# Loading and preparing a pair's q and k three steps sooner, and giving v a norm and a scale of its own, in a fused attention and two-stage MoE kernel

## The chip, the core and the metric

The kernel runs on one core of a Trainium2 chip. The metric is the time of one execution in microseconds (us), and lower is better. The core's engines are TensorE (PE in the profile, with PEld for its weight loads), VectorE (DVE), ScalarE (ACT), GpSimd (POOL) and SyncE (SP). Each runs its own instructions in the order in which they were issued. SP and POOL mostly start transfers (DMAs) here.

## The reference, cut to what matters

```python
B, H, S, D = 4, 8, 576, 64
q_rot, k_rot = rotate(q), rotate(k)                 # rope
scores = q_rot @ k_rot.T / sqrt(D)                  # 576 x 576 for each of 32 heads
attn = softmax(scores)
x = (attn @ v)                                      # -> 2304 tokens x 512
h = x @ w_in; x = leaky(h) @ w_out                  # dense MoE stage, 512 -> 2048 -> 512
logits = normalize(x) @ normalize(expert_emb).T / tau
out = gate * relu(x @ w1[e]) @ w2[e]                # second stage, one of 8 experts per token
```

All inputs and outputs are float32. The kernel reaches that precision by splitting numbers into a high and a low part (float16 or a rounded float32) and adding the products. To fit float16, a tensor is first scaled by a power of two, which is found from its sum of squares.

## The kernel before

**Pairs, units and steps.** Two heads make a pair, and there are 16 pairs (`g`), four for each batch. A pair is cut into nine units (`u`), blocks of query rows. One call of `step(i)` issues one step: the scores of unit i+1 (`a_scores`, lines 570 to 574), the maximum of unit i (`a_max`, line 579), the exponential and the two parts of P of unit i-1 (`a_exp` 584, `a_hi` 588, `a_lo` 592), the transpose of that P by a DMA on SP's queue (`a_transpose`, line 596, tile PT), and the product with v of unit i-4 (`a_pv`, line 631). The first four pairs (`WHOLE`) are computed in full float32 and transpose with PE instead; pairs 4 to 15 are split, and only they have `prep`, `prep_v` and the DMA transposes.

**The dense stage in between.** Once x of two blocks of 128 tokens is complete, units of the dense stage are issued in the same steps: `m_s1` (line 256, one in every second step) and `m_s2` (line 286) in the step after it. A block's x gets there by `x_done`: a square on ACT, a power of two on DVE, two halves `x16` (lines 684 and 686) and a DMA transpose on SP's queue (line 690, tiles xT and xt). After attention the rest of the dense stage, the routing and the experts follow.

**Preparing a pair.** `load(g, 2)` brings q and k of a pair (640 KB) by one DMA on POOL's queue into the only buffer `raw2`; `load(g, 1)` brings v (320 KB) into `raw1`. `prep(g)` is a list of pieces:

- the squares of q, k and v (line 461, ACT) with rope (lines 389, 392, 396, DVE);
- `total` (line 186), a PE product with ones that adds the three sums over the partitions;
- `_pow2` (lines 91 to 93) and two small products (lines 470, 471) on DVE, which give the scales;
- the high parts (line 482, ACT) and the low parts (line 486, DVE) with one copy (line 512) into `stg`;
- a DMA transpose of `stg` into `stk` on SP's queue (line 515), and two DMAs of 80 KB on POOL's queue that copy q's rows into `zq` (line 523). These wait for the transpose, and behind them on POOL's queue stands `load(g + 1, 2)`.

`prep_v(g)` then makes v's high and low parts (lines 535, 537) with the third scale of the same `_pow2`, copies them to other partitions by two DMAs of 130 and 162.5 KB on POOL's queue (lines 540, 541), and issues `load(g + 1, 1)` behind them.

**What sets the order.** With i0 = 9 (g - 1), the step at which the pair before begins, the first piece of `prep(g)` may run from step i0 - EARLY, and at the soonest TLOAD = 4 steps after its load was issued. The transpose into `stk` may run from step i0 - 1. `prep_v`'s first piece runs from step i0 + LAG = i0 + 4. `slot` takes the pieces of the waiting jobs: x_done first, then prep, prep_v, routing, and weights last. A step has two such places (four before the dense stage begins), with one piece of a job in each; a job that changes its engine, or that needs PE, waits for the next step. `prep(g)` is created only when both its q and k and its v have been asked for.

Of the kernel before, what the change touches and what calls it, by code (L numbers as in the profile page):

```python
# [9 lines left out]
F32 = mybir.dt.float32  # L10
# [32 lines left out]
BUR = 1.5
WARM = 9
# [39 lines left out]
            self.run()  # L84


def _pow2(nc, pool, sq2, n, inv):

    t = pool.tile([128, n], U32, name="pt", tag=f"pt{n}")
    s = pool.tile([128, n], F32, name="ps", tag=f"ps{n}")  # L90
    nc.vector.tensor_scalar(out=t, in0=sq2.bitcast(U32), scalar1=0xFFFFFFFF, scalar2=24, op0=ALU.bitwise_xor, op1=ALU.logical_shift_right)
    nc.vector.tensor_scalar(out=s.bitcast(U32), in0=t, scalar1=-50.0, scalar2=2.0 ** 23, op0=ALU.add, op1=ALU.mult)
    nc.vector.tensor_scalar(out=inv.bitcast(U32), in0=t, scalar1=-2.0 ** 23, scalar2=304.0 * 2 ** 23, op0=ALU.mult, op1=ALU.add)
    return s


# [1 line left out]
def attention_moe_kernel(ctx: ExitStack, tc: tile.TileContext, qkv, w_in, w_out, emb, tau, w1, w2,  # L98
                         rope, ident, tokc, iota, pcol, out):
    nc = tc.nc  # L100
# [66 lines left out]
    M = Ctx()  # L167
# [36 lines left out]
    def weights(i):  # L204
        while len(slices) > (SPARE if i >= NW else 0):
            f, o = slices.popleft()
            if i < NW:
                raw = wp.tile([128, 512, 2], U32, name=f"raw{i}")
            else:
                raw = mp.tile([128, 8, 256], F16, name="xT", bufs=XTB).rearrange("p a b -> p (a b)").bitcast(U32).rearrange("p (f t) -> p f t", t=2)  # L210
            if o:
                nc.sync.dma_start(out=raw.rearrange("p f t -> p (f t)"), in_=w_out32[128 * f:128 * f + 128, :])
                r = yield from decode(raw)
                yield Piece(A=0.75, when=lambda: f in M.scaled)
                nc.scalar.activation(out=wo[:, 0, f], in_=r, func=AF.Copy, scale=uw[:, f:f + 1])
                yield Piece(V=0.6)
                nc.vector.scalar_tensor_tensor(out=wo[:, 1, f], in0=r, scalar=uw[:, f:f + 1], in1=wo[:, 0, f].bitcast(F32), op0=ALU.mult, op1=ALU.subtract)
            else:
                nc.sync.dma_start(out=raw.rearrange("p (c f) t -> p c (f t)", c=4),
                                  in_=w_in32[:, 256 * f:256 * f + 256].rearrange("(c p) f -> p c f", p=128))  # L220
                w = yield from decode(raw)
                sq = small.tile([128, 1], F32, name="wsq", bufs=NW)
                yield Piece(A=0.86)
                nc.scalar.activation(out=junk[:, 0:512], in_=w, func=AF.Square, accum_out=sq, saturate=False)
                pb = yield from total(sq, 1)
                yield Piece(must=True, V=0.2)
                s = _pow2(nc, small, pb[:, 0:1], 1, uw[:, f:f + 1])
                M.scaled.add(f)
                hi = wi[:, 0, :, 128 * f:128 * f + 128]
                wv = w.rearrange("p (c f) -> p c f", c=4)  # L230
                yield Piece(A=0.75)
                nc.scalar.activation(out=hi, in_=wv, func=AF.Copy, scale=s)
                yield Piece(V=0.6)
                nc.vector.scalar_tensor_tensor(out=wi[:, 1, :, 128 * f:128 * f + 128], in0=wv, scalar=s, in1=hi, op0=ALU.mult, op1=ALU.subtract)
            M.wdone[o].add(f)
            yield Piece()
# [119 lines left out]
        nc.gpsimd.memset(e[:, S:640], 0.0)  # L356
    tab = qkp.tile([128, 2, 5, 64], F32, name="tab")
    raws = {}
    pairs, values = {}, {}
    xrow = {}  # L360

    def load(g, z):
        raws[g, z] = qkp.tile([128, z, 5, 2, 64], F32, name=f"raw{z}")
        for t in ([slice(0, 2)] if g else [slice(0, 1), slice(1, 2)]) if z == 2 else [slice(2, 3)]:
            if z == 2:
                M.loaded = M.tick
            if (g, z, t.start) == (0, 2, 1):
                nc.sync.dma_start(out=tab, in_=rope)
            (nc.gpsimd if g else nc.sync).dma_start(out=raws[g, z][:, t.start % 2:t.start % 2 + t.stop - t.start], in_=qkv[g, :, t])
# [84 lines left out]

    def prep(g):
        i0 = 9 * (g - 1)
        raw, rawv = raws.pop((g, 2)), raws.pop((g, 1))[:, 0]
        sq = small.tile([128, 3], F32, name="sq3")

        def square(t):  # L460
            nc.scalar.activation(out=junk, in_=(raw[:, t] if t < 2 else rawv).rearrange("p c h d -> p (c h d)"), func=AF.Square, accum_out=sq[:, t:t + 1], saturate=False)

        by_head = raw.rearrange("p t c h d -> p t h c d")

        m3 = small.tile([128, 3], F32, name="m3")
        sc = small.tile([128, 2], F32, name="sc")

        def scales(pb):
            s3 = _pow2(nc, small, pb[:, 0:3], 3, m3)
            nc.vector.scalar_tensor_tensor(out=sc[:, 0:1], in0=m3[:, 0:1], scalar=0.125, in1=m3[:, 1:2], op0=ALU.mult, op1=ALU.mult)  # L470
            nc.vector.tensor_scalar(out=sc[:, 1:2], in0=sc[:, 0:1], scalar1=-1.0, scalar2=None, op0=ALU.mult)
            return s3
# [19 lines left out]
        yield Piece(A=0.93, V=0.85)  # L492
        square(1)
        rope_s(1)
        yield Piece(A=0.93, V=1.5)
        square(2)
        rope_c(0)
        rope_c(1)
        yield Piece(V=1.4)
        add(slice(0, 2))  # L500
        pb = yield from total(sq, 3)
        yield Piece(must=True, V=0.6)
        s3 = scales(pb)
        s2, qhi, khd, qlo, klo = stacks()
# [5 lines left out]
        yield Piece(V=1.3)  # L510
        lo(klo, 1, khd[:, :, :, 0:64])
        nc.vector.tensor_copy(out=khd[:, :, :, 64:128], in_=khd[:, :, :, 0:64])
        yield Piece(at=i0 - 1)
        stk = stp.tile([128, 5, 640], F16, name="stk")
        nc.sync.dma_start_transpose(out=stk.rearrange("p s (c x) -> p (s c) x", c=5), in_=s2)
# [6 lines left out]
            for h in range(2):  # L522
                nc.gpsimd.dma_start(out=zq[g % 2][64 * h:64 * h + 64, h, 0:640], in_=stk[64 * h:64 * h + 64, h])
        pairs[g] = (stk, s3, sc, zq[g % 2] if zq else None)
        if g + 1 < 4 * B:
            load(g + 1, 2)
        vjobs.append(Job(prep_v(g, rawv, s3)))

    def prep_v(g, rawv, s3):
        yield Piece(A=0.82, at=9 * (g - 1) + LAG)  # L530
        v16 = values[g] = stp.tile([128, 9, 2, 130], F16, name="v16", tag="v")
        nc.gpsimd.memset(v16[:, 0:5, :, 128:130], 1.0)
        vh, vl = (v16[:, 0:5, :, o:o + 64].rearrange("p c h d -> p (c h) d") for o in (64, 0))
        rv = rawv.rearrange("p c h d -> p (c h) d")
        nc.scalar.activation(out=vh, in_=rv, func=AF.Copy, scale=s3[:, 2:3])
        yield Piece(V=0.75)
        nc.vector.scalar_tensor_tensor(out=vl, in0=rv, scalar=s3[:, 2:3], in1=vh, op0=ALU.mult, op1=ALU.subtract)
        yield Piece()

        nc.gpsimd.dma_start(out=v16[0:64, 5:9], in_=v16[64:128, 0:4])  # L540
        nc.gpsimd.dma_start(out=v16[64:128, 4:9], in_=v16[0:64, 0:5])
        if g + 1 < 4 * B:
            load(g + 1, 1)
# [89 lines left out]

    def a_fin(g, u, o):
        b, p = divmod(g, 4)
        s3 = pairs[g][1]
        c = u // 2
        r = slice(0, 128) if c < 4 else slice(64 * (b % 2), 64 * (b % 2) + 64)
        if c == 4 and b % 2:
# [8 lines left out]
        if g < WHOLE:  # L648
            nc.vector.tensor_scalar(out=rd[r], in0=ov[r, :, 64:65], scalar1=1e-9, scalar2=None, op0=ALU.add)
        else:  # L650
            nc.vector.tensor_scalar(out=rd[r], in0=ov[r, :, 64:65], scalar1=EPS_P, scalar2=s3[r, 2:3], op0=ALU.add, op1=ALU.mult)
        nc.vector.reciprocal(out=rd[r], in_=rd[r])
        nc.vector.tensor_tensor(out=x[r, 128 * p:128 * p + 128].rearrange("p (h d) -> p h d", h=2), in0=ov[r, :, 0:64],
                                in1=rd[r].to_broadcast([n, 2, 64]), op=ALU.mult)
# [17 lines left out]
    def x_done(b, c, x):  # L672
# [1 line left out]
        ch = chunk[b, c]  # L674
        j = block_of[b, c]
        yield Piece(A=0.61, when=lambda: not any(z.live for z in wjobs[NW:]) and j < cur_block() + (2 * XTB if decoded() else XTB))
        sq = small.tile([128, 1], F32, name="xsq")
        nc.scalar.activation(out=junk[:, 0:512], in_=x, func=AF.Square, scale=2.0 ** 0.5, accum_out=sq, saturate=False)
        yield Piece(V=0.5)
        s = _pow2(nc, small, sq, 1, ux[:, ch:ch + 1])  # L680
# [16 lines left out]

    def directions():

        en2 = small.tile([NE, 1], F32, name="en2")  # L700
        warm = small.tile([128, 1], F32, name="warm")
# [341 lines left out]
    L.prep, L.x, L.fin, L.o = None, -1, None, None  # L1043

    def jobs():
        if (L.prep is None or not L.prep.live) and preps and all((preps[0], z) in raws for z in ((2,) if preps[0] < WHOLE else (1, 2))):
            L.prep = Job((prep_whole if preps[0] < WHOLE else prep)(preps.popleft()))
        for q in (xjobs, vjobs, rjobs):
            while q and not q[0].live:
                q.popleft()  # L1050
        return [z for z in [*list(xjobs)[:2], L.prep, *list(vjobs)[:1], *list(rjobs)[:1], *wjobs] if z is not None and z.live]
# [350 lines left out]
```

## Time and profile before

| what | value |
|---|---|
| three timed runs | 1005.59, 1006.17 and 1009.71 us, median 1006.17 us |
| the profiled execution | 1004.24 us |
| its span, from the first instruction to the last | 1002.5 us |
| mean granted clock of TensorE | 0.984 of full speed |
| busy share of the span | PE 92%, DVE 77%, PEld 76%, ACT 67%, POOL 11% |

The span is what the profile's views divide up; 1.7 us of the execution lie around it. A wait that a view names is idle time of one engine, and it costs time only where that engine, or one that waits for it, sets the pace.

### The profile page before, as it was taken

To read this page: it belongs to the slowest core of one execution; us is meant where nothing else is said; L and a number is where in the kernel's file an instruction comes from. 1 tells how busy PE (TensorE), PEld (TensorE's weight loads), DVE (VectorE), ACT (ScalarE), POOL (GpSimd) and SP (SyncE) were. 2 spreads that over 40 slices of the span, in tenths; PEclk is the share of its full clock that TensorE was granted. 3 is DMA by queue.
4 is the path that set the end of the run, shared out by engine and by line. 5 is a ranking of instruction groups with operands and counts; after the bars stand their busy time and mean duration, and the time that the engine had idled before them with its cause. 6 is when DMAs were issued, how large, how long until landed. Compare 5 with 4: busy or idle time off the path is not lost. (4 is left out here: it accounts for less than half of the span.)

```text
span 1002.5 us, 20186 instructions
## 1 busy us (share of the span) xinstructions
PE 922.8 (92%) x7428; PEld 762.3 (76%) x7428; DVE 774.6 (77%) x1632; ACT 671.0 (67%) x1081; POOL 114.8 (11%) x157
## 2 busy tenths in 40 slices
PE   2788977899996999998899999999999999999997
PEld 1677766577885788887778888888877788888885
DVE  5988887787888889888778766322668999999993
ACT  5888888555676866667566655333155998888883
POOL 0000000001101100110100100000012351111111
PEclk9999999899998999999989999999999999999999
DMA  6435442969889998977957744101323111116190
GB/s 233 140 108 164 158 137 65 131 110 146 159 131 165 180 151 140 176 142 133 173 110 138 155 77 86 40 22 33 127 85 106 55 42 53 43 43 211 40 358 25
DMA packets 219848, 120.09 MB, mean 120 GB/s; under 512 B 194711, under 2 KB 203159, under 8 KB 219744
## 3 DMA queue, kind: packets, MB, share of 16 engines
q1 hardware_dynamic: 210000, 84.54, 40.4%
q0 software_dynamic: 9744, 34.21, 13.0%
q8 instruction: 60, 0.98, 0.4%
q14 instruction: 44, 0.36, 0.1%
HBM read 120.04 MB, written 10.49 MB: 130 GB/s over the span
## 5 line engine op out<-in xcount | busy, mean ns | idle before, releaser
L256 PEld LDWEIGHTS <-wi 128*128 128x128 f16 x1920 | 170.4, 98 | 28.0 <-issue 7.3
L286 PE MATMUL acc<-wo,gh 128*128 128x512 f32 x576 | 154.6, 411 | 6.0 <-ACT gh L270 6.0
L263 ACT ACTIVATE g<-h 128x512 f32<-128x512 f32 x72 | 43.0, 597 | 138.3 <-DVE gl L274 64.4
L286 PEld LDWEIGHTS acc<-wo,gh 128*128 128x128 f32 x576 | 105.4, 192 | 30.6 <-ACT gh L270 8.4
L579 DVE TENSOR_SCALAR_CACHE_REDUCE E<-S,sc 128x576 f32<-128x576 f32 x108 | 87.9, 814 | 45.7 <-PE S L572 33.3
L584 ACT ACTIVATE E<-E,amx 128x576 f32<-128x576 f32 x144 | 110.5, 767 | 16.9 <-DVE E L579 16.1
L256 PE MATMUL h<-xT,wi 128*128 128x256 f16 (+1 forms) x1152 | 112.0, 255 | 2.5 <-DMA xT<-x 2.5
L256 PE MATMUL h<-xt,wi 128*128 128x256 f16 x768 | 89.9, 274 | 0.9 <-DMA xt<-x 0.9
L588 ACT ACTIVATE P<-E 128x576 f16<-128x576 f32 x108 | 73.8, 684 | 20.5 <-DMA PT<-P 17.4
L592 DVE SCALAR_TENSOR_TENSOR P<-E,P 128x576 f16<-128x576 f32 x108 | 81.0, 750 | 7.6 <-ACT P L588 7.3
L631 PEld LDWEIGHTS <-PT 128*128 128x128 f16 (+1 forms) x1680 | 61.9, 101 | 25.1 <-issue 15.7
L286 PE MATMUL acc<-wo,gl 128*128 128x512 f32 x288 | 78.9, 397 | 0.0
L631 PE MATMUL o<-v,PT 128*128 128x65 f16 (+3 forms) x1680 | 70.5, 195 | 7.2 <-DMA PT<-P 7.2
L274 DVE TENSOR_TENSOR gl<-g,gh 128x512 fp32r<-128x512 f32 x72 | 49.5, 687 | 31.5 <-ACT gh L270 21.3
L266 DVE SCALAR_TENSOR_TENSOR g<-h,g 128x512 f32<-128x512 f32 x72 | 49.5, 687 | 23.8 <-ACT g L263 23.4
L570 PE MATMUL S<-stk 128*128 128x288 f16 (+1 forms) x240 | 60.6, 292 | 7.5 <-DVE E L579 7.5
L286 PEld LDWEIGHTS acc<-wo,gl 128*128 128x128 f32 x288 | 55.2, 192 | 12.4
L1001 PE MATMUL h<-w,hth 128*128 128x512 f32 x176 | 55.3, 395 | 0.4 <-ACT hth L985 0.4
L270 ACT ACTIVATE gh<-g 128x512 fp32r<-128x512 f32 x72 | 44.5, 618 | 16.6 <-PE acc L286 13.2
L935 DVE TENSOR_TENSOR w<-rb,w 128x1024 fp32r<-128x1024 f32 x40 | 46.3, 1221 | 3.4 <-ACT w L934 2.6
L572 PE MATMUL S<-stk,zq 128*128 128x288 f16 (+1 forms) x200 | 48.6, 289 | 0.0
L631 PE MATMUL o<-v,ET 128*128 128x65 f32 (+1 forms) x400 | 47.0, 269 | 0.0
(273 smaller groups left out, 1980.8 us busy)
## 6 DMA issues: line engine op xcount, KB each, us to landing
rb<-in_w SPq DMA_DIRECT2D x78, 512.0 KB
ra<-in_w SPq DMA_DIRECT2D x76, 512.0 KB
raw<-in_qkv POOLq DMA_DIRECT2D x15, 640.0 KB, 6.1
raw<-in_w_in SPq DMA_DIRECT2D x13, 512.0 KB
raw<-in_w_out SPq DMA_DIRECT2D x13, 512.0 KB
x2s<-x POOLq DMA_DIRECT2D x18, 256.0 KB, 4.5
raw<-in_qkv POOLq DMA_DIRECT2D x12, 320.0 KB, 9.2
v<-v POOLq DMA_DIRECT2D x12, 162.5 KB, 8.1
```

Of the source, the lines that this page charges most:

```text
L256: nc.tensor.matmul(m.h[:, c0:c1], lhsT=wi[:, a, c, 128 * f:128 * f + 128], rhs=xT[j][:, 4 * b_ + c, 0:c1 - c0], start=(n == 0), stop=(n == ...
L266: nc.vector.scalar_tensor_tensor(out=m.g, in0=m.h, scalar=0.01, in1=m.g, op0=ALU.mult, op1=ALU.max)
L274: nc.vector.tensor_tensor(out=m.gl, in0=m.g, in1=m.gh.bitcast(F32), op=ALU.subtract)
L286: nc.tensor.matmul(M.acc[:, t], lhsT=g_[:, tt], rhs=wo[:, a, f], start=(f == 0 and n == 0), stop=(f == NF - 1 and n == 2))
L570: nc.tensor.matmul(ps[o:o + m, n, 0:288], lhsT=stk[:, h, c0:c0 + m], rhs=stk[:, 2 + h, ks], start=True, stop=False)
L572: nc.tensor.matmul(ps[o:o + m, n, 0:288], lhsT=pairs[g][3][:, h, c0:c0 + m], rhs=stk[:, 4, ks], start=False, stop=True)
L579: nc.vector.tensor_scalar(out=e[:, 0:S].rearrange("p (a b) -> p a b", a=2), in0=ps[:, :, 0:288], scalar1=-0.125 if g < WHOLE else pairs[g] ...
L584: nc.scalar.activation(out=e[:, 0:S], in_=e[:, 0:S], func=AF.Exp, scale=-1.0, bias=mx)
L588: nc.scalar.activation(out=p[:, 0:576], in_=e[:, 0:S], func=AF.Copy, scale=TWO15)
L592: nc.vector.scalar_tensor_tensor(out=p[:, 576:1152], in0=e[:, 0:S], scalar=TWO15, in1=p[:, 0:576], op0=ALU.mult, op1=ALU.subtract)
L631: nc.tensor.matmul(o[ob:ob + m, 256 * h:256 * h + w], lhsT=pt[:, i, q0:q0 + m], rhs=v[:, j, h, c:c + w], start=(n == 0), stop=(n == len(to ...
L1001: nc.tensor.matmul(OP[kk], lhsT=h_[:, c, :], rhs=wt[a][c // 2][:, 512 * (c % 2):512 * (c % 2) + 512], start=(n == 0), stop=(n == len(todo) ...
```

## The change

Four things change. EARLY goes from 2 to 5. `load(g + 1, 2)` is issued right after the last piece that reads `raw2`, ahead of the transpose into `stk` and of the `zq` copies. The square, the sum and the power of two of v leave `prep` and become the first pieces of `prep_v`, from step i0 + 1, with a `total` and a two-instruction `_pow2` of their own. And `prep(g)` no longer needs v to have been asked for.

```diff
-EARLY = 2
+EARLY = 5
-def _pow2(nc, pool, sq2, n, inv):
+def _pow2(nc, pool, sq2, n, inv, own=""):
...
-    nc.vector.tensor_scalar(out=inv.bitcast(U32), in0=t, scalar1=-2.0 ** 23, scalar2=304.0 * 2 ** 23, op0=ALU.mult, op1=ALU.add)
+    if inv is not None:
+        nc.vector.tensor_scalar(out=inv.bitcast(U32), in0=t, scalar1=-2.0 ** 23, scalar2=304.0 * 2 ** 23, op0=ALU.mult, op1=ALU.add)
...
             if z == 2:
                 M.loaded = M.tick
+            else:
+                M.loaded_v = M.tick
...
-        raw, rawv = raws.pop((g, 2)), raws.pop((g, 1))[:, 0]
-        sq = small.tile([128, 3], F32, name="sq3")
+        raw = raws.pop((g, 2))
+        sq = small.tile([128, 2], F32, name="sq2")
...
-            s3 = _pow2(nc, small, pb[:, 0:3], 3, m3)
+            s3 = _pow2(nc, small, pb[:, 0:2], 2, m3)
...
-        yield Piece(A=0.93, V=1.5)
-        square(2)
+        yield Piece(V=1.5)
         rope_c(0)
         rope_c(1)
         yield Piece(V=1.4)
         add(slice(0, 2))
-        pb = yield from total(sq, 3)
+        pb = yield from total(sq, 2)
...
         nc.vector.tensor_copy(out=khd[:, :, :, 64:128], in_=khd[:, :, :, 0:64])
+        if g + 1 < 4 * B:
+            load(g + 1, 2)
         yield Piece(at=i0 - 1)
         stk = stp.tile([128, 5, 640], F16, name="stk")
...
-        if g + 1 < 4 * B:
-            load(g + 1, 2)
-        vjobs.append(Job(prep_v(g, rawv, s3)))
+        vjobs.append(Job(prep_v(g)))
-    def prep_v(g, rawv, s3):
+    def prep_v(g):
+        yield Piece(A=0.93, at=9 * (g - 1) + LAG - 3, tick=M.loaded_v + TLOAD, when=lambda: (g, 1) in raws)
+        rv = raws.pop((g, 1))[:, 0].rearrange("p c h d -> p (c h d)")
+        sq = small.tile([128, 1], F32, name="vsq", tag="sq1", bufs=NW)
+        nc.scalar.activation(out=junk, in_=rv, func=AF.Square, accum_out=sq, saturate=False)
+        pb = yield from total(sq, 1)
+        yield Piece(must=True, V=0.4)
+        s3 = scale_v[g] = _pow2(nc, small, pb[:, 0:1], 1, None, "v")
...
-            nc.vector.tensor_scalar(out=rd[r], in0=ov[r, :, 64:65], scalar1=EPS_P, scalar2=s3[r, 2:3], op0=ALU.add, op1=ALU.mult)
+            nc.vector.tensor_scalar(out=rd[r], in0=ov[r, :, 64:65], scalar1=EPS_P, scalar2=scale_v[g][r], op0=ALU.add, op1=ALU.mult)
...
-        if (L.prep is None or not L.prep.live) and preps and all((preps[0], z) in raws for z in ((2,) if preps[0] < WHOLE else (1, 2))):
+        if (L.prep is None or not L.prep.live) and preps and all((preps[0], z) in raws for z in (2,)):
```

The rest of the diff shares out the small tiles' buffers anew.

## Rows read from the trace of the kernel before

**Rows 1.** The page's first part: busy time of each engine over the span.
```profile
PE 922.8 (92%) x7428; PEld 762.3 (76%) x7428; DVE 774.6 (77%) x1632; ACT 671.0 (67%) x1081; POOL 114.8 (11%) x157
```

**Rows 2.** Busy time by stretch: PE, PEld, DVE, ACT, POOL, then clock, DMA share, GB/s.
```profile
185.00:200.00 15.00, 12.35 (x91) 8.66 (x90) 7.94 (x16) 8.38 (x13) 1.60 (x3) 0.77 1.15 161
225.00:250.00 25.00, 25.00 (x226) 18.87 (x223) 19.32 (x41) 12.96 (x23) 3.33 (x7) 1.00 0.96 152
300.00:327.00 27.00, 18.98 (x186) 14.72 (x184) 23.11 (x58) 17.16 (x33) 3.88 (x8) 0.84 1.02 167
495.00:510.00 15.00, 9.86 (x70) 7.52 (x69) 7.59 (x14) 6.05 (x11) 0.09 (x1) 0.77 0.78 119
545.00:550.00 5.00, 5.00 (x44) 4.04 (x43) 4.57 (x15) 4.21 (x7) 0.00 (x0) 1.00 0.36 68
```

**Rows 3.** Timeline from 481 to 502 us: start, length, instruction, idle time before it.
```profile
481.39 1.05 POOL L523 DMA_DIRECT2D zq<-stk  x2 [20.34 <-DMA stk<-stg]
482.51 0.57 POOL L369 DMA_DIRECT2D raw<-in_qkv  x1
...
486.98 0.57 POOL L369 DMA_DIRECT2D raw<-in_qkv  x1
...
500.96 0.59 PE L631 MATMUL o<-v,PT 128*128 128x65 f16 x14 [3.45 <-DMA PT<-P]
501.00 0.68 ACT L588 ACTIVATE P<-E 128x576 f16<-128x576 f32 x1 [6.61 <-DMA PT<-P]
```

**Rows 4.** Timeline from 180 to 190 us: a load, a transpose and a late xT.
```profile
180.49 1.28 SPq L690 DMA_TRANSPOSE xT<-x  x1
180.77 0.54 POOL L369 DMA_DIRECT2D raw<-in_qkv  x1 [30.08 <-issue]
...
181.88 7.85 SPq L515 DMA_TRANSPOSE stk<-stg  x1
...
189.26 0.72 ACT L684 ACTIVATE x<-x,ps 128x512 f16<-128x512 f32 x1 [4.74 <-DMA xT<-x]
```

**Rows 5.** Line 515's instructions: shortest, median and longest in ns, first and last start.
```profile
L515 SPq DMA_TRANSPOSE stk<-stg x12: 3143/3346/7853, 137.1 to 553.8; - x12
```

**Rows 6.** The view of waits: total us, times, longest.
```profile
ACT P L588 <- DMA PT<-P: 17.4, 8, 6.6
...
PE o L631 <- DMA PT<-P: 7.2, 3, 3.5
DVE pt L91 <- PE t L186: 5.8, 6, 2.3
```

**Rows 7.** Timeline of PE, a step with a `total` and one without.
```profile
391.25 0.58 PE L631 MATMUL o<-v,PT 128*128 128x65 f16 x14
391.67 0.36 PE L186 MATMUL t<-sq,ones 128*128 128x3 f32 x2
391.90 0.28 PE L570 MATMUL S<-stk 128*128 128x288 f16 x1
...
398.69 0.58 PE L631 MATMUL o<-v,PT 128*128 128x65 f16 x14
399.11 0.29 PE L570 MATMUL S<-stk 128*128 128x288 f16 x1
```

**Rows 8.** Groups by line: busy us, mean ns of one, idle time before and its releaser.
```profile
L92 DVE TENSOR_SCALAR ps<-pt 128x1 uint32<-128x1 uint32 (+1 forms) x46 | 7.3, 158 | 1.6
```

**Rows 9.** Timeline of pair 11: first square, transpose, first maximum.
```profile
380.97 0.72 ACT L461 ACTIVATE junk<-raw 128x640 fp8e4<-128x640 f32 x1
...
401.31 3.40 SPq L515 DMA_TRANSPOSE stk<-stg  x1
...
426.12 0.81 DVE L579 TENSOR_SCALAR_CACHE_REDUCE E<-S,sc 128x576 f32<-128x576 f32 x1
```

**Rows 10.** Timeline from 317 to 328 us: a wait for PT and the dense stage's restart.
```profile
317.41 0.59 PE L631 MATMUL o<-v,PT 128*128 128x65 f16 x14 [3.17 <-DMA PT<-P]
...
327.10 1.22 PE L256 MATMUL h<-xt,wi 128*128 128x256 f16 x5 [0.23 <-DMA xt<-x]
```

More of the change, by code (lines that the diff above doesn't have):

```diff
@@ L84, in finish @@
             self.run()
-def _pow2(nc, pool, sq2, n, inv):
-    t = pool.tile([128, n], U32, name="pt", tag=f"pt{n}")
-    s = pool.tile([128, n], F32, name="ps", tag=f"ps{n}")
+def _pow2(nc, pool, sq2, n, inv, own=""):
+    t = pool.tile([128, n], U32, name="pt", tag=f"pt{own}{n}")
+    s = pool.tile([128, n], F32, name="ps", tag=f"ps{own}{n}", bufs=6 if n == 1 and not own else 3)
     nc.vector.tensor_scalar(out=t, in0=sq2.bitcast(U32), scalar1=0xFFFFFFFF, scalar2=24, op0=ALU.bitwise_xor, op1=ALU.logical_shift_right)
     nc.vector.tensor_scalar(out=s.bitcast(U32), in0=t, scalar1=-50.0, scalar2=2.0 ** 23, op0=ALU.add, op1=ALU.mult)
-    nc.vector.tensor_scalar(out=inv.bitcast(U32), in0=t, scalar1=-2.0 ** 23, scalar2=304.0 * 2 ** 23, op0=ALU.mult, op1=ALU.add)
+    if inv is not None:
+        nc.vector.tensor_scalar(out=inv.bitcast(U32), in0=t, scalar1=-2.0 ** 23, scalar2=304.0 * 2 ** 23, op0=ALU.mult, op1=ALU.add)
     return s
@@ L221, in weights @@
                 w = yield from decode(raw)
-                sq = small.tile([128, 1], F32, name="wsq", bufs=NW)
+                sq = small.tile([128, 1], F32, name="wsq", tag="sq1", bufs=NW)
                 yield Piece(A=0.86)
@@ L358, in attention_moe_kernel @@
     raws = {}
-    pairs, values = {}, {}
+    pairs, values, scale_v = {}, {}, {}
     xrow = {}
@@ L456, in prep @@
         i0 = 9 * (g - 1)
-        raw, rawv = raws.pop((g, 2)), raws.pop((g, 1))[:, 0]
-        sq = small.tile([128, 3], F32, name="sq3")
+        raw = raws.pop((g, 2))
+        sq = small.tile([128, 2], F32, name="sq2")
         def square(t):
-            nc.scalar.activation(out=junk, in_=(raw[:, t] if t < 2 else rawv).rearrange("p c h d -> p (c h d)"), func=AF.Square, accum_out=sq[:, t:t + 1], saturate=False)
+            nc.scalar.activation(out=junk, in_=raw[:, t].rearrange("p c h d -> p (c h d)"), func=AF.Square, accum_out=sq[:, t:t + 1], saturate=False)
         by_head = raw.rearrange("p t c h d -> p t h c d")
-        m3 = small.tile([128, 3], F32, name="m3")
+        m3 = small.tile([128, 2], F32, name="m2")
         sc = small.tile([128, 2], F32, name="sc")
         def scales(pb):
-            s3 = _pow2(nc, small, pb[:, 0:3], 3, m3)
+            s3 = _pow2(nc, small, pb[:, 0:2], 2, m3)
             nc.vector.scalar_tensor_tensor(out=sc[:, 0:1], in0=m3[:, 0:1], scalar=0.125, in1=m3[:, 1:2], op0=ALU.mult, op1=ALU.mult)
@@ L524, in prep @@
         pairs[g] = (stk, s3, sc, zq[g % 2] if zq else None)
-        if g + 1 < 4 * B:
-            load(g + 1, 2)
-        vjobs.append(Job(prep_v(g, rawv, s3)))
-    def prep_v(g, rawv, s3):
+        vjobs.append(Job(prep_v(g)))
[7 more added lines that the diff above has]
+        s3 = scale_v[g] = _pow2(nc, small, pb[:, 0:1], 1, None, "v")
+        rv = rv.rearrange("p (c d) -> p c d", d=64)
         yield Piece(A=0.82, at=9 * (g - 1) + LAG)
@@ L533, in prep_v @@
         vh, vl = (v16[:, 0:5, :, o:o + 64].rearrange("p c h d -> p (c h) d") for o in (64, 0))
-        rv = rawv.rearrange("p c h d -> p (c h) d")
-        nc.scalar.activation(out=vh, in_=rv, func=AF.Copy, scale=s3[:, 2:3])
+        nc.scalar.activation(out=vh, in_=rv, func=AF.Copy, scale=s3)
         yield Piece(V=0.75)
-        nc.vector.scalar_tensor_tensor(out=vl, in0=rv, scalar=s3[:, 2:3], in1=vh, op0=ALU.mult, op1=ALU.subtract)
+        nc.vector.scalar_tensor_tensor(out=vl, in0=rv, scalar=s3, in1=vh, op0=ALU.mult, op1=ALU.subtract)
         yield Piece()
@@ L635, in a_fin @@
         b, p = divmod(g, 4)
-        s3 = pairs[g][1]
         c = u // 2
@@ L676, in x_done @@
         yield Piece(A=0.61, when=lambda: not any(z.live for z in wjobs[NW:]) and j < cur_block() + (2 * XTB if decoded() else XTB))
-        sq = small.tile([128, 1], F32, name="xsq")
+        sq = small.tile([128, 1], F32, name="xsq", tag="sq1", bufs=NW)
         nc.scalar.activation(out=junk[:, 0:512], in_=x, func=AF.Square, scale=2.0 ** 0.5, accum_out=sq, saturate=False)
@@ L698, in directions @@
     def directions():
-        en2 = small.tile([NE, 1], F32, name="en2")
-        warm = small.tile([128, 1], F32, name="warm")
+        en2 = small.tile([NE, 1], F32, name="en2", bufs=1)
+        warm = small.tile([128, 1], F32, name="warm", bufs=1)
         nc.scalar.activation(out=warm, in_=ones[:, 0:1], func=AF.Sqrt)
```

## The prediction

> **What bounds the kernel now.** I read the page first: PE is busy for 92% of the span and the next engine, DVE, for 77% [rows 1]. But the shares are means over stages, so I went on to busy time by stretch [rows 2]. Where dense units run between the attention steps, PE has no idle time at all (25.00 of 25 us from 225) while DVE works 19.3 us and ACT 13.0. There only PE work counts. The third thing to see in those rows is the DMA share: 0.96 there, against 0.36 from 545 to 550, a stretch where little but the PT transposes moves. The DMA engines are thus nearly full on average, and above 1 in bursts.
>
> The stretches in which PE does idle are the ones a schedule change can reach. Three matter [rows 2]. From 185 to 200 PE lacks 15.00 - 12.35 = 2.65 us, and the clock is 0.77 on average, a part of it at the lower level (1.2 of 2.4 GHz) after PE stood still; 0.23 of 15 us is 3.45 us more, 6.1 in all. From 495 to 510 it is 5.14 + 3.45 = 8.6 us. From 300 to 327 it is 8.0 us of idleness and 0.16 of 27 = 4.3 of clock, but most of this has another cause: no dense unit is ready until x of batch 1 has been transposed [rows 10], and DVE, at 23.1 of 27 us, sets the pace. The view of waits names one kind of wait common to these places: ACT's next P and PE's product with v wait for a PT transpose, 17.4 us in 8 waits and 7.2 us in 3 [rows 6].
>
> The timeline says why [rows 3]. Within 6 us POOL issues the zq copies (160 KB), q and k of the next pair (640 KB), v's copies (292 KB) and the next v (320 KB), right behind the transpose into stk. The PT transposes share the DMA engines with this burst; some 14 us after its start ACT has waited 6.61 us and PE 3.45 for one of them. The chain of waits that the page follows back from the end shows only the last store and is of no use here.
>
> Last, is the preparation itself late? No [rows 9]. Pair 11's preparation begins at 380.97, its stk transpose is issued at 401.31, and its first maximum is at 426.12. That leaves 24.8 us for a transpose of 3.4 and two copies. So starting three steps sooner removes no wait for stk. What it can do is move loads and vector work.
>
> **The change part by part.** A step takes 3.7 us (the products with v at 391.25 and 398.69 are two steps apart [rows 7]).
>
> *Added.* Each of the 12 split pairs gets one more `total`. On PE it costs the difference between a step with one and a step without: 391.90 - 391.25 = 0.65 against 399.11 - 398.69 = 0.42, so 0.23 us; 12 x 0.23 = +2.8 us, not hidden where PE is the bound. From below it is 0, if all fell where PE idles; from above it is the whole pair of products, 0.36 us, 12 x 0.36 = +4.3. On DVE come two small instructions a pair, 0.16 us each by the like of them [rows 8], 12 x 0.32 = 3.8 us; in the PE-bound stretches DVE has 5.7 of 25 us free, so I take 0 (without this cover, +3.8). The new `_pow2` must run at the head of a step and can hold DVE until PE has made the sum; behind it in DVE's order stands the maximum of the step, and PE's next scores wait for that. The trace has 5.8 us of this in 6 waits, and one `total` for each of 12 pairs and 16 weight slices, 28 in all: 0.2 us each, and 12 x 0.2 = 2.5 us of DVE. I take +0.5, between 0 and 2.5. The square of v is moved, not added. Sum +3.3 (0 to 10.6).
>
> *Moved: the preparation.* The same ACT and DVE pieces run three steps sooner. For the whole pairs and the first split one the guard of four steps after the load leaves little or nothing of this: pairs 1 to 3 cannot start sooner, pair 4 by one step, pair 5 by two. From pair 6 on I count: start at i0 - 5, last low part and the load at i0 - 1, transpose at i0; the load's guard then allows i0 + 3, and the next start is due at i0 + 4. So the rhythm holds. In PE-bound stretches DVE and ACT hide the move: 0. Between 300 and 327 about as many pieces enter DVE's load as leave it: 0, with 2.5 us either way, two pieces by the costs that the code gives them (V=0.85 to 1.5).
>
> *Moved: the loads.* On POOL's queue the 640 KB of q and k now stand before the zq copies instead of behind them, and the whole sequence load, stk, zq comes three steps (11 us) sooner than v's copies and v's load, which stay at i0 + 5. The burst splits in two: 640 + 160 KB with the stk transpose, then 292 + 320 KB. Nothing else is queued behind the load on POOL that anyone waits for, and the load waits only for DVE's last read of raw2.
>
> For the stall at 495 this takes away 800 of the 1412 KB that go before it. At the 161 GB/s of a full stretch [rows 2] these are 5.0 us of transfer, more than PE's wait of 3.45 and less than ACT's of 6.61 [rows 3]. So PE's wait should go, and the low clock with it, while a rest of ACT's may stay: I take 7.5 of the 8.6 us as saved (0 to 8.6). The stall at 185 is another case: a load issued at 180.77, the stk transpose at 181.88 held for 7.85 us, and an xT, issued just before both, that kept ACT waiting 4.74 us [rows 4]. Load and transpose move two steps sooner there and miss that xT, but they can meet the one before, for which the first dense units wait. I take half, -3.0 (-6.1 to +4). From 300 to 327 PE waits 3.17 us for a PT at 317 and the dense stage restarts at 327 [rows 10]; without that wait I count -3.2, and against it +1.7, my estimate, half of it, because pair 9's stk and pair 10's load now fall among the xt transposes: -1.5 (-5 to +4).
>
> *The price of the new place.* Pair 5's sequence at 180 is the order of the new kernel: load, then stk at once. The transpose then held SP's queue for 7.85 us against a median of 3.35 [rows 5], 4.5 us more, and behind it stand the PT transposes. A PT is needed three steps, 11 us, after its issue. So 4.5 us are mostly covered. Where x transposes or stores join, the cover is gone. I take +1.5 in all; the upper bound is the 2.5 us or so of an average wait (17.4 / 8 = 2.2 [rows 6], and PE less) in each of the nine pairs 6 to 14, +20.
>
> The Trainium skill bears on this in "DMA: Bandwidth & Descriptors", section "Issuing engines are not separate DMA queues": transfers started by SP and by GpSimd end up on the same 16 DMA engines and interleave. It speaks against the change, since another queue gives the load no bandwidth of its own; the 7.85 us in [rows 4] agree with it. By it alone the bytes per pair stay the same and a collision is only moved, which gives the second case below.
>
> *Sum.* +3.3 - 7.5 - 3.0 - 1.5 + 1.5 = -7.2 us. Against the profiled execution, 1004.24, this is 997.0. The median of the timed runs is 1.9 above that execution, so I expect 999.
>
> **The rivals.** *Collisions are only moved.* The bursts get smaller, but stk with the load in front reaches xT and PT about as often as the old burst did; for it speaks the DMA share near 1 in all stretches but the late ones. The gains of 12 us shrink to 3 or 4 and the added PE work cancels them: 1003 to 1009, about 1006.
>
> *Slower: SP's queue is held in every pair.* If each stk takes 7.85 us from pair 6 on and the PTs behind it come later than their 11 us, PE and ACT stop once a pair, and the clock falls after it as in the two stretches at 0.77 [rows 2]. The point that decides is a PT landing more than 7 us later than now. With 1.5 us lost in nine pairs, the work of +3.3 and no gain: 1006.2 + 13.5 + 3.3 - some 6 for the old stalls that go = 1017. Against it: behind the 7.85 us at 181.88 the wait was ACT's for xT, not one for PT [rows 4].
>
> *The change does not act.* If the guard or the order of jobs holds the start of the preparation where it was, only the additions are left: 1006.2 + 3.3 = 1009.5. My count of steps speaks against it.
>
> **How the numbers follow.** 0.5% (5 us) is about what a measurement of this kernel can tell from no change. Chances: relief 0.50, with a range of its own from 991 to 1005; collisions moved 0.30; SP's queue held 0.14; not acting 0.06. Faster by over 0.5% (below 1001.1): 0.36 of the relief and 0.09 of the moved collisions, since which transposes they meet is decided by a step either way; 0.45. Slower by over 0.5% (above 1011.2): 0.12 of the held queue, 0.02 of the case that does not act and 0.03 of the moved collisions; 0.17. The rest is 0.38. The range leaves out about one in ten on each side. Below, the three stalls gone with the additions as estimated: 1006.2 - 8.6 - 6.1 - 5 + 3.3 = 990. Above, halfway from no relief (1009.5) to the held queue (1017): 1013.
>
> **What would show it.** In the profile of the changed kernel: q and k's load issued some 11 us sooner against the attention steps, and ahead of line 523; line 515 with a median near 7 us if the load slows it, near 3.4 if not; waits of ACT and PE for PT well below 17.4 and 7.2 us; no stretch with a clock of 0.77 near 500; 24 more products on line 186, two for each sum of v. The prediction is wrong if PT waits stay as long, or if PE idles at each pair's stk.

## The result, and the profile after

The change made the kernel slower: a median of 1012.12 us (1008.68 to 1016.32, 20 runs) against 1007.47 (998.86 to 1016.29, 20 runs) for the kernel before on the same chips, a ratio of 1.0064 with a 95% interval from 1.0045 to 1.0083. The ratios compare fast executions alone, and four of the kernel before, more than 1.5% above its fastest, are left out. The prediction was 999.0, faster than before; the range of 990 to 1013 holds the measured time, near its upper end. The profiled execution took 1011.73 us (span 1009.9, mean clock 0.979). Line numbers of the new kernel differ: the transpose into stk is line 519 (before 515), the load 372 (369), the `zq` copies 527 (523), `total` 187 (186).

The page of the new kernel begins:

```profile
PE 932.9 (92%) x7452; PEld 764.8 (76%) x7452; DVE 777.5 (77%) x1656; ACT 671.0 (66%) x1081; POOL 113.8 (11%) x155
```

PE has the 24 added products (7428 to 7452, [rows 1]), and its busy time grew by 10.1 us, of which 24 products of 0.25 us explain 6.0. POOL issues two instructions fewer: the two `zq` copies of one pair are gone.

The view of waits of the new kernel (total us, times, longest):

```profile
DVE pt L91 <- PE t L187: 20.6, 13, 6.1
...
ACT P L597 <- DMA PT<-P: 11.7, 6, 4.3
...
PE h L257 <- DMA xt<-x: 7.3, 2, 6.8
...
ACT x L692 <- DMA xt<-x: 5.7, 2, 4.4
```

Against [rows 6], ACT's wait for PT fell from 17.4 to 11.7 us and that of PE's products (7.2 us) is gone from the view. In its place DVE waits for a `total` (5.8 to 20.6 us), and PE and ACT wait for xt, PE for 6.8 us in one go.

Busy time by stretch of the new kernel (columns as in [rows 2]):

```profile
185.00:200.00 15.00, 14.97 (x141) 11.37 (x139) 14.83 (x34) 11.45 (x20) 1.60 (x3) 1.00 0.41 86
225.00:250.00 25.00, 25.00 (x218) 18.38 (x216) 22.59 (x52) 13.36 (x21) 2.13 (x4) 1.00 0.64 94
301.00:342.00 41.00, 26.54 (x247) 20.26 (x246) 28.29 (x73) 22.12 (x40) 3.70 (x7) 0.79 0.79 147
...
508.00:523.00 15.00, 14.89 (x143) 12.29 (x141) 12.68 (x30) 12.38 (x22) 0.55 (x1) 1.00 0.91 192
```

The stall near 500 is gone: the steps that follow unit 116's maximum, at 494.9 before and at 509.2 now, run with PE at 14.89 of 15 us and the clock at 1.00. But from 301 to 342 PE lacks 14.5 us. The same steps of the kernel before, from the maximum of unit 67 to that of unit 75, lacked 8.1:

```profile
300.18:332.20 32.02, 23.90 (x249) 18.71 (x248) 27.64 (x70) 22.11 (x42) 3.88 (x8) 0.84 0.92 152
```

The most useful reading is the length of each pair, from its first maximum to the next pair's, taken from the maxima in the timelines (us):

| pair | 4 | 5 | 6 | 7 | 8 | 9 | 10 | 11 | 12 | 13 | 14 |
|---|---|---|---|---|---|---|---|---|---|---|---|
| before | 45.2 | 38.7 | 36.3 | 34.8 | 36.2 | 33.7 | 35.6 | 36.2 | 43.4 | 37.8 | 32.2 |
| after | 41.0 | 39.0 | 40.6 | 39.0 | 41.6 | 35.5 | 35.8 | 37.3 | 39.2 | 35.9 | 32.8 |
| after less before | -4.2 | 0.3 | 4.3 | 4.2 | 5.4 | 1.8 | 0.2 | 1.1 | -4.2 | -1.9 | 0.6 |

The relief is there, 10.3 us in pairs 4, 12 and 13. Pair 6 loses 4.3, pairs 7 and 8 lose 9.6, the others 4.0. The table compares one execution with one. In two executions of one kernel (e4y and f3 below) pair 8 took 41.3 and 35.2 us, so pair 8's 5.4 would not be shown by the table alone; the stretch from unit 67 to unit 75, read below, differs by 2.1 us between those two.

**Pair 6.** The last weight slice and pair 6's stk in the kernel before:

```profile
201.74 0.75 DVE L217 SCALAR_TENSOR_TENSOR wo<-raw,uw,wo 128x512 fp32r<-128x512 f32 x1
...
222.02 4.13 SPq L515 DMA_TRANSPOSE stk<-stg  x1
```

The timeline of the new kernel, first around the last weight slice, then the scores of a unit of pair 6 and of one of pair 10:

```profile
207.51 5.48 SPq L519 DMA_TRANSPOSE stk<-stg  x1
...
211.94 0.74 DVE L218 SCALAR_TENSOR_TENSOR wo<-raw,uw,wo 128x512 fp32r<-128x512 f32 x1
...
247.03 0.33 DVE L523 MEMSET zq<- 64x320 uint32 x1
...
270.36 0.28 PE L579 MATMUL S<-stk 128*128 128x288 f16 x1
270.58 0.29 PE L583 MATMUL S<-stk 64*128 64x288 f16 x1
270.80 0.30 PE L579 MATMUL S<-stk 128*128 128x288 f16 x1
271.03 0.29 PE L583 MATMUL S<-stk 64*128 64x288 f16 x1
...
388.48 0.29 PE L579 MATMUL S<-stk 128*128 128x288 f16 x1
388.60 0.29 PE L581 MATMUL S<-stk,zq 128*128 128x288 f16 x1
388.72 0.29 PE L579 MATMUL S<-stk 128*128 128x288 f16 x1
388.85 0.29 PE L581 MATMUL S<-stk,zq 128*128 128x288 f16 x1
```

`zq`, a copy of q's 64 rows that is padded with zeros to 128, takes the buffers of the weight stage. So it is made only when `decoded()` holds (line 516 before), that is, when the last weight slice has been issued, and that is decided by the order in which work is issued. Before, the last slice came ahead of pair 6's stk. Now stk comes 14.5 us sooner and the slice 10.2 us later, so pair 6 goes without `zq`, and its second products use 64 rows. Each product then starts 0.22 us after the one before instead of 0.12. A pair has 20 products of each kind: 40 x 0.10 = 4.0 us of the 4.3.

**Pairs 7 and 8.** The timeline of the new kernel where the dense stage restarts:

```profile
325.24 5.88 SPq L519 DMA_TRANSPOSE stk<-stg  x1
...
325.43 0.54 POOL L372 DMA_DIRECT2D raw<-in_qkv  x1 [10.06 <-DVE stg L514]
...
332.59 1.31 SPq L698 DMA_TRANSPOSE xt<-x  x1
...
335.92 4.50 PE L257 MATMUL h<-xt,wi 128*128 128x256 f16 x24 [6.84 <-DMA xt<-x]
...
335.96 0.72 ACT L692 ACTIVATE x<-x,ps 128x512 f16<-128x512 f32 x1 [4.40 <-DMA xt<-x]
```

Pair 9's stk, slowed to 5.88 us, stands with one PT in front of the xt with which the dense stage restarts, pair 10's load runs beside it, and PE waits 6.84 us for that xt. From the maximum of unit 67 to that of unit 75 it now takes 40.2 us (before 32.0). In the kernel before, pair 9's stk came behind the restart at 327.10 [rows 10]:

```profile
333.39 4.21 SPq L515 DMA_TRANSPOSE stk<-stg  x1
```

**The transpose into stk** (line 519: shortest, median, longest in ns), in the new kernel, median 5.5 us against 3.3 in [rows 5]:

```profile
L519 SPq DMA_TRANSPOSE stk<-stg x12: 3767/5494/10696, 132.7 to 550.8; - x12
```

With the load put back behind stk the median is 4.0 us (e2 below). The load that slows it is issued by another engine, so the other queue did not keep the two apart. This agrees with the Trainium skill, "DMA: Bandwidth & Descriptors", section "Issuing engines are not separate DMA queues", which says that transfers started by different engines run on the same 16 DMA engines.

### The profile page after: what moved, and what is told of

The parts are those of the page before. It is cut to its first block, busy times and chain, and to the rows that moved or that the text cites. A ratio compares the mean times of both kernels' runs of the same rounds, so it can differ in the third digit from the quotient of the medians.

```text
span 1009.9 us, 20260 instructions
## 1 busy us (share of the span) xinstructions
PE 932.9 (92%) x7452; PEld 764.8 (76%) x7452; DVE 777.5 (77%) x1656; ACT 671.0 (66%) x1081; POOL 113.8 (11%) x155
## 5 line engine op out<-in xcount | busy, mean ns | idle before, releaser
L257 PE MATMUL h<-xT,wi 128*128 128x256 f16 (+1 forms) x1152 | 114.6, 258 | 3.0 <-DMA xT<-x 3.0
L597 ACT ACTIVATE P<-E 128x576 f16<-128x576 f32 x108 | 73.9, 684 | 14.9 <-DMA PT<-P 11.7
L640 PEld LDWEIGHTS o<-v,ET 128*128 128x128 f32 (+1 forms) x400 | 44.6, 186 | 0.8 <-issue 0.7
```

Source lines behind the costliest of these rows:

```text
L257: nc.tensor.matmul(m.h[:, c0:c1], lhsT=wi[:, a, c, 128 * f:128 * f + 128], rhs=xT[j][:, 4 * b_ + c, 0:c1 - c0], start=(n == 0), stop=(n == ...
L597: nc.scalar.activation(out=p[:, 0:576], in_=e[:, 0:S], func=AF.Copy, scale=TWO15)
L640: nc.tensor.matmul(o[ob:ob + m, 256 * h:256 * h + w], lhsT=pt[:, i, q0:q0 + m], rhs=v[:, j, h, c:c + w], start=(n == 0), stop=(n == len(to ...
```

## The experiments

Every ratio is to the kernel before, run on the same chip, with its 95% interval. Two kernels were run a second time: e4y as f3 (0.9872 and 0.9844) and e25y as f4 (0.9897 and 0.9891), which shows how well ratios repeat.

### Undoing the losses one by one

**e1: pair 6 waits for the last weight slice**, and so has `zq`.

```diff
-        yield Piece(at=i0 - 1)
+        yield Piece(at=i0 - 1, when=lambda: g != 6 or decoded())
```

> The changed kernel, with one edit: pair 6's transpose into stk may only be issued once the last weight slice is decoded, so that pair 6 has its zq tile again. Theory Z: pair 6 gets back to about 36.5 us, and of the 6.5 us over before some 4 go: +2.5 us. Rival (the zq tile does not matter, or the later transpose costs as much): +6.5 us as now, or more.

Ratio 1.0018 [0.999, 1.0046], 0.46% below the change. Pair 6 is 35.6 us long.

**b1: the kernel before, without `zq` for pair 6.**

```diff
-        if not zq and decoded():
+        if not zq and decoded() and g > 6:
```

> The kernel before, with one change: pair 6 gets no zq tile, as in the changed kernel, and its second score products use 64 rows. Theory Z (the lost zq tile of pair 6 is a part of the loss): the nine units of pair 6 take some 0.45 us longer each, pair 6 from first maximum to first maximum of pair 7 goes from 36.4 to about 40.4 us, and the time is 4 us (0.4%) longer than before. Rival (pair 6 is slower in the changed kernel because of transfers or of the added sums, and the form of the score products does not matter): no difference from before, 0 +- 1 us.

Ratio 1.0077 [1.0046, 1.0107]; pair 6 grows from 36.3 to 40.5 us. Its profile also has longer PT waits (ACT 28.5 us) and a pair 8 of 42.7, so not all of its 0.77% is `zq`.

**e2: the load goes back behind stk and `zq`.**

```diff
-        if g + 1 < 4 * B:
-            load(g + 1, 2)
         yield Piece(at=i0 - 1)
...
         pairs[g] = (stk, s3, sc, zq[g % 2] if zq else None)
+        if g + 1 < 4 * B:
+            load(g + 1, 2)
```

> The changed kernel, with the load of the next q and k put back behind the transpose into stk and the zq copies; preparation still starts at i0 - 5. Theory S1 (the load in front of it is what makes the stk transpose hold SP's queue, and near 330 us this makes the second xt late and the dense stage's restart with it): stk's median falls from about 6 or 7 us to 3.3, PE's wait of 6.84 us for xt falls below 3, and 3 to 6 of the 6.5 us go. Theory S2 (it is the place of pair 9's transpose among the xt transposes, whatever stands in front): the wait for xt stays at 5 to 7 us and the time at +5 to +7 us. Theory Z has no effect here: pair 6 has no zq tile in this kernel either.

Ratio 1.0031 [1.0004, 1.0057], 0.33% below the change. The median stk falls to 4.0 us and no wait of ACT or PE for a PT is left in the view of waits. The wait for xt at the restart stays:

```profile
PE h L257 <- DMA xt<-x: 5.0, 2, 4.7
...
ACT x L692 <- DMA xt<-x: 3.4, 2, 2.3
```

**e5: pair 9's preparation starts when it did before.**

```diff
-at=max(i0 - EARLY, 0)
+at=max(i0 - (2 if g == 9 else EARLY), 0)
```

> The changed kernel, but pair 9 alone, whose preparation falls into the restart of the dense stage, starts at i0 - 2 again (its load of pair 10 and its transpose come three steps later). Theories S1 and S2: the xt transposes no longer stand behind stk, PE's wait of 6.84 us goes to below 2 us, the restart comes one step sooner, and some 5 us of the 6.5 go: +1.5 us. Rival (the starved stretch is longer because the steps in it are longer, by pieces on DVE and by the sums): under 2 us go, +5 us or more.

Ratio 1.0003 [0.9976, 1.003], 0.61% below the change. From unit 67 to 75 it takes 33.1 us (40.2 in the changed kernel, 38.0 in e2), and PE's wait for xt is 2.0 us in all.

**e15 = e1 + e5, e12 = e1 + e2, e125 = all three.**

> The changed kernel with both repairs: pair 6's transpose waits for the last decoded weight slice (it has its zq tile again), and pair 9's preparation starts at i0 - 2. If the two losses are separate, their gains add: 1.0064 - 0.0046 - 0.0061 = 0.996, 4 us faster than before, with pair 6 at about 35.6 us and the stretch from unit 67 to unit 75 (32.0 us before, 40.2 us in the changed kernel) at about 33. Rival (pair 9 given back its place only looked like a gain because another collision moved, or the repairs get in each other's way): 0.999 to 1.003.

> The changed kernel, with pair 6's zq tile back (its transpose waits for the last decoded slice) and the load of q and k behind the transpose, but pair 9 started early as in the change. The three kernels with these edits so far gave 1.0031 (load behind alone), 1.0018 (zq tile alone) and 0.9892 (these two and pair 9 late). If the losses add, zq's 0.0046 comes off 1.0031: 0.9985, and pair 9's place alone is worth 0.009. If the stretch from unit 67 to 75 is again 33 us or less although pair 9 starts early, then only the load in front was to blame there: 0.990.

> The changed kernel with both repairs, and with the load of the next q and k behind the transpose and the zq copies again. If the load in front of the transpose costs by itself, by holding SP's queue in each pair, this is another 1 to 3 us faster than with the two repairs alone: 0.993 to 0.995. If the load in front only mattered at the dense stage's restart, where pair 9 now no longer collides: the same as the two repairs, 0.996 +- 0.001.

e15 1.0001 [0.9971, 1.0031], e12 0.9934 [0.9906, 0.9963], e125 0.9892 [0.9851, 0.9932]. All three edits together take 1.7% off the changed kernel. How much of it belongs to each depends on which of the others is in place:

- pair 6's wait: 0.46% alone, 0.97% with the load behind (e2 to e12);
- the load's place: 0.33% alone, 0.84% behind e1;
- pair 9's edit: 0.61% alone, 0.17% behind e1, 0.42% behind e12.

With intervals of 0.3 to 0.4% on each side of a ratio, the gains of 0.33, 0.17 and 0.42% are not clear of zero, and no split of the 1.7% among the three is shown. e15 missed the 0.996 that separate losses would give. In e12 pair 9 starts early and the stretch from unit 67 to 75 takes 34.2 us, so the load's place counts there too. The load's place is not one cause alone: with the load later, the guard of four steps makes the next preparation later as well. In e125 stk is issued 22.5 to 25.5 us ahead of its pair's first maximum from pair 9 on, as before (22.0 to 29.6), and not 30.0 to 41.4 as in the changed kernel. The repairs thus take most of the early start back.

### The halves apart

**e4: v's own sum alone** (EARLY at 2, load behind as in e2). **e4y: e4 with `zq` as soon as the buffers are free.** **e4z: e4 with e1's wait.**

```diff
-        if not zq and decoded():
+        if not zq and not slices and not (wjobs[0].live or wjobs[1].live):
```

> One part of the change alone: v has a sum and a power of two of its own, while EARLY is 2 and the load is behind the transpose, as before. In this order too the last weight slice is decoded after pair 6's transpose, so pair 6 gets no zq tile. If the cost of the part is PE's time for 12 sums plus the lost zq tile: 2.8 + 4.4 = 7 us over before (1.007). If the loss of the zq tile is owed to the early start and not to v's own sum: pair 6 has its tile and the time is 1.003.

> v's own sum alone (EARLY 2, load behind), and the zq tiles made as soon as the two weight buffers that they take are free, without any wait: pairs 5 and 6 have zq tiles too, 11 pairs instead of 9 of the same kernel without this edit, which was at 0.9965. Theory Z: 4.4 us for pair 6 and up to as much for pair 5: 0.988 to 0.992. If the 0.9965 was luck of the order and not the transfers kept apart, other pairs lose it again: 0.995 to 1.000.

> The same part alone, and pair 6's transpose waits for the last decoded slice, so that pair 6 has its zq tile. Estimate from PE alone: 12 sums at 0.23 us, +2.8 us over before (1.003). Rival (a wait of DVE for v's sum stands in front of each step's maximum, 20.6 us in 13 waits in the changed kernel, and costs by itself): +6 us or more (1.006).

e4 0.9965 [0.9933, 0.9997], although it too loses pair 6's `zq` (last slice at 226.91, stk at 220.89) and has a pair 6 of 40.6 us. ACT's PT waits fall to 3.4 us and pair 12 to 38.2 us. e4y 0.9872 [0.9829, 0.9916], with `zq` for pairs 5 and 6 (34.0 and 35.6 us). e4z came out at 1.0059 [1.0022, 1.0096] and says nothing of v's sum: with its wait every later preparation is late too. From pair 7 on stk is issued 10.6 to 14.9 us ahead of its pair's first maximum, against 22.0 to 29.6 before, and ACT stood still for loads, here for 8.08 us:

```profile
405.22 0.74 ACT L464 ACTIVATE junk<-raw 128x640 fp8e4<-128x640 f32 x1 [8.08 <-DMA raw<-in_qkv]
```

**e25y: the change with the load behind, pair 9 late, and e4y's `zq`.**

> The changed kernel with the load behind, pair 9 late, and zq tiles from pair 6 on by the free buffers instead of a wait; against the kernel with v's own sum alone it shows what the early start itself is worth. Estimate: 0.989, as with all three repairs. If the early start brings nothing once the losses are repaired, it is no faster than v's own sum alone with zq tiles, which has one more pair with them; if it brings the relief near 185 us, its pair 4 is 2 to 4 us shorter.

0.9897 [0.9863, 0.9932].

**f1: the early start alone** (the kernel before with EARLY at 5). **f2: e4y's `zq` alone** in the kernel before. **f3 = e4y and f4 = e25y** beside them on one chip.

> The kernel before with EARLY at 5 and nothing else: v's square stays in the preparation of q and k, the load stays behind stk and zq. Theory A (v's square couples the two: v's load comes last in the burst, and a preparation that begins sooner finds it missing): the early start cannot act or waits for raw in ACT; the PT waits stay near 17 us or turn into waits for v's load, ratio 0.998 to 1.01. Theory B (the early start is what relieves the bursts): PT waits well below 17 us, the stall near 500 gone, ratio 0.985 to 0.995.

> The kernel before, with zq made as soon as the weights' buffers are free instead of when the last weights are split; nothing else is changed. Theory A (the relief comes from v's own sum, and zq for pair 5 as well is worth 4 to 5 us at the most): ratio 0.993 to 1.000, the PT waits stay. Theory B (the gain of the version with v's sum and zq is that of zq alone): ratio 0.985 to 0.99.

> Only v's own sum, load behind stk, EARLY at 2, zq by free buffers: the kernel that measured 0.9872 before, beside f4 on one chip. Theory A (the early start adds nothing): 0.985 to 0.991, within 0.003 of f4. Theory B (the early start adds its own gain): 0.004 or more above f4.

> Both parts of the change, with the load behind stk, pair 9's preparation late and zq by free buffers: the kernel that measured 0.9897 before, beside f3 on one chip. Theory A (the early start adds nothing): 0.986 to 0.992, within 0.003 of f3. Theory B: 0.004 or more below f3.

f1 0.9901 [0.9869, 0.9932], f2 0.9965 [0.9932, 0.9998], f3 0.9844 [0.9812, 0.9877], f4 0.9891 [0.9864, 0.9918]. f1 refutes what I believed after e4 and b2 (below), that v's square in the preparation makes an early start useless: the early start alone gains 1.0%, and this without pair 6's `zq` (40.5 us). f3 against f4: with both parts the kernel is no faster than with v's sum alone; f4 has `zq` from pair 6, f3 from pair 5. f1 and e2 differ in v's own sum and in what comes with it (the preparation no longer needs v); both have the early start, the load behind stk and no `zq` for pair 6. e2 is 1.3% slower than f1, so the two halves hinder each other.

**g1: f1 with e4y's `zq`.**

> The kernel before with EARLY at 5 and zq by free buffers; v's square stays in the preparation of q and k, the load stays behind stk and zq. Theory A (either half separates the load of q and k from v's copies, and that is the gain; zq for pair 6 adds 4 to 5 us): ratio 0.984 to 0.988, as the version with v's own sum alone. Theory B (v's own sum gives something that the early start cannot): 0.989 or more.

0.9835 [0.9795, 0.9876], median 993.28 us against 1010.58 for the kernel before; pair 6 is 36.0 us long. g1 has `zq` from pair 6, as the kernel before has. So either half alone, with `zq`, is faster than the kernel before: the early start by 1.6%, v's own sum by 1.3 and 1.6% (e4y and f3, where pair 5 has `zq` as well). This measurement can't tell g1 from f3 (991.16 us against 1008.22).

### What the halves have in common

Both halves put some time between the load of q and k and v's copies, which in the kernel before are issued almost together. POOL's rows in the timelines of f1 (copies on line 540), f3 (549) and the changed kernel (549):

```profile
406.16 0.56 POOL L369 DMA_DIRECT2D raw<-in_qkv  x1
...
411.99 0.53 POOL L540 DMA_DIRECT2D v<-v  x1 [4.60 <-ACT E L584]
412.52 0.52 POOL L541 DMA_DIRECT2D v<-v  x1
413.03 0.56 POOL L369 DMA_DIRECT2D raw<-in_qkv  x1
```

```profile
477.25 0.57 POOL L372 DMA_DIRECT2D raw<-in_qkv  x1
...
481.88 0.53 POOL L549 DMA_DIRECT2D v<-v  x1 [3.39 <-issue]
```

```profile
474.95 0.54 POOL L372 DMA_DIRECT2D raw<-in_qkv  x1 [7.74 <-DVE stg L514]
...
505.56 0.53 POOL L549 DMA_DIRECT2D v<-v  x1 [13.14 <-DVE P L601]
```

From pair 6 to pair 14 the distance from load to copies is 1.0 to 4.0 us before, 4.3 to 9.5 us in f3 and g1 and 23.5 to 30.6 in the changed kernel. **b2 and g2** open it in the kernel before, by two steps and by one (the edit of g2 is shown), and do nothing else:

```diff
-        yield Piece(A=0.82, at=9 * (g - 1) + LAG)
+        yield Piece(A=0.82, at=9 * (g - 1) + LAG + 1)
```

> The kernel before, with one edit and no added work: v's preparation, with its copies and the next v's load, may start two steps later (i0 + 6). Theory B (in the kernel before, the q and k load, v's copies and v's load follow one another within 6 us, and this burst is what makes PT transposes late): ACT's 17.4 us of waits for PT fall below 8, the stall from 495 to 510 goes, and the time falls by 4 to 8 us, 0.992 to 0.996. Rival (the total of the transfers is what counts, not their spacing): 1.000 +- 0.003, with the waits moved to other places.

> The kernel before with prep_v one step (3.7 us) later, so that v's copies and v's load follow the load of q and k by some 4 to 6 us instead of 0.5 to 3.4; nothing else is changed. Theory A (the distance is the cause): the PT waits of ACT fall from 17.4 to below 9 us, pair 12 is 38 to 40 us long instead of 43.4, and v's load is late for the square by less than with two steps (below 8 us in all): ratio 0.990 to 0.998. Theory B (the distance is not the cause): PT waits of 14 us or more, pair 12 above 42 us, ratio 0.998 to 1.005.

g2 0.9958 [0.9926, 0.999]: ACT's wait for PT falls from 17.4 to 3.0 us and pair 12 from 43.4 to 39.3. b2 1.0024 [0.9987, 1.0061]: 17.4 to 6.9, pair 12 39.1, but pair 13 grows from 37.8 to 42.1. The distance does relieve the transposes. Neither edit gains what the halves gain. v's load is now later, and ACT's square in the preparation waits for it, 20.5 us in g2 and 17.9 in b2; that this is the whole reason is not shown. The views of waits of g2, g1 and f3:

```profile
ACT junk L461 <- DMA raw<-in_qkv: 20.5, 10, 6.8
...
ACT P L588 <- DMA PT<-P: 3.0, 2, 2.7
```

```profile
ACT junk L461 <- DMA raw<-in_qkv: 7.0, 7, 1.7
...
DVE pt L91 <- PE t L186: 4.2, 6, 1.3
...
ACT P L588 <- DMA PT<-P: 1.5, 2, 1.2
```

```profile
DVE pt L91 <- PE t L187: 9.0, 15, 1.3
...
ACT junk L464 <- DMA raw<-in_qkv: 2.4, 2, 1.7
...
ACT P L597 <- DMA PT<-P: 2.2, 1, 2.2
```

In g1 and f3 no wait of the three kinds is longer than 2.2 us. In the changed kernel ACT waits 11.7 us for PT in spite of a distance of 28 us in the median, and not at all in e2, where the load stands behind stk. So the PT transposes there most likely meet the load in front of stk; e2's later preparations were not tried apart from it.

The timelines also show how early the early start is. Counted in units, stk is issued 5 units ahead of its pair's first maximum in the kernel before and in f3, 6 (once 7) in f1 and g1, and 7 to 9 in the changed kernel, from pair 6 on. So "the early start alone" moves stk by one step and not by three.

## Why the prediction was wrong

Two steps failed above all. The sum has no term for `zq`, where pair 6 lost 4.3 us, and it counted -1.5 us for the restart of the dense stage, where the steps took 8.2 us more. The relief that it forecast came, and these losses outweigh it.

**Right.** The stall near 500 went, with the low clock; PT waits of PE went and ACT's fell; q and k's load came ahead of the `zq` copies, and the median stk, 5.5 us, lies between the two values I named; 24 products were added. The relief at the two stalls is 10.3 us against the 10.5 forecast: 4.2 in pair 4 for my 3.0, and 6.1 in pairs 12 and 13 for my 7.5. Pair 13, which begins at 505.7 in the kernel before, belongs to the second stall: from 505 to 510 PE is busy throughout, at a mean clock of 0.54:

```profile
505.00:510.00 5.00, 5.00 (x27) 3.71 (x27) 2.81 (x5) 2.89 (x5) 0.00 (x0) 0.54 0.24 45
```

In e2, with no wait for a PT at all, pairs 12 and 13 take 73.0 us together, 81.3 before, so some 8 of the 8.6 were to be had. One reading was off, without effect on the sum: the waits of 6.61 and 3.45 us in [rows 3] end some 20 us after the burst's first copy, not 14.

**The term that is missing: `zq`.** The sum moves stk sooner and puts weight slices last, but never asks what `decoded()` answers at that point. Pair 6 became 4.3 us longer, and giving it `zq` back gained 0.46% (e1). Either half alone loses it too (e4, f1).

**"From 300 to 327 ... -1.5".** The mechanism was named, pair 9's stk and pair 10's load among the xt transposes, and priced at +1.7, +4 at the most for the stretch. The stretch from unit 67 to 75 became 8.2 us longer, and 7.1 of these went when pair 9 alone started late (e5). I took half of a PT wait as the price; what waited was the one transpose with which the dense stage restarts, and PE had no other dense work. This is the collision that the rival "collisions are only moved" spoke of, at about 1006 us.

**"The price of the new place ... +1.5".** Moving the load back gave 0.33% (e2) and, from e1 to e12, 0.84%, some 3 and 8 us. Part of it is the later preparation, so the size of the queue's part alone stays open. The rival "SP's queue is held in every pair" gave 1017 us, nearer than my forecast, but by PT waits in each pair, and those fell.

**"Moved: the loads".** This step took the split of the burst as the fruit of the load's new place. Either half alone splits it with the load where it was, and g2, with a median distance of 7.0 us for the 2.7 of before, shows that some 4 us more are enough for the PT waits. The changed kernel, with a median of 28 us, still waits 11.7 us for PT.

**"Added ... +3.3".** The price of 12 sums stays open. f3, with them, is as fast as g1, without, but f3 also has `zq` for pair 5 (34.0 us, in g1 38.4), so a price of 3.3 us would not be seen. DVE's waits for `total` rose by 14.8 us, where the sum had 2.5 us of DVE and priced them at +0.5. They rise that far only with both halves together (4.4 in f1, 9.0 in f3, 18.5 in e2), and what they cost was not measured.

**Open.** Why the halves hinder each other. Without `zq` for pair 6, with the load behind stk, both halves (e2) are 1.3% slower than the early start alone (f1). The stretch from unit 67 to 75, 38.0 us against 32.3, is 5.7 us of some 13. The rest, DVE's waits and the stk that comes up to two units sooner among it, was not taken apart. With all repairs the two are still at 0.989 (f4), either half alone at 0.984 (g1, f3). `zq` for pair 5 (4.9 us between f4 and f3) may account for f3 but not for g1, which lacks it as f4 does. Nor was v's sum taken out of f3 with the distance kept.

## What to carry to other kernels

When work moves in a static schedule, list every condition that is answered while instructions are issued (a buffer that another stage frees, a last slice): a move can silently choose a slower form of later work, and the first sign is an instruction count. In g2 a few microseconds between the parts of a burst took most of its waits away, so try the smallest move first, and each half of a change alone. Price a moved transfer by the one consumer that has nothing else to do, here the first dense unit of a batch, and not by the average wait.

## What the runs showed of the hardware

Score products of 128 x 288 that alternate between 128 and 64 rows of weights start 0.22 us apart, and 0.12 us apart when the 64 rows are padded with zeros to 128, with the same 0.29 us each. In this kernel a padded copy, which needs two more DMAs, is worth about 4 us a pair (pair 6: 36.3 us with it, 40.5 without in b1). The DMA transpose into stk, 3.3 us in the median, took 5.5, and up to 10.7, with a load of 640 KB issued beside it from another engine, and 4.0 with that load behind it (e2).
